# Seven wide block products for two token groups of the GLU layer, and all attention beside the first group

## The chip, the cores and the metric

One core of a Trainium2 chip runs the whole program. The metric is the device time of one execution in microseconds (us); less is better. The kernel before takes 665.15 us (median of 3 runs, 665.14 to 665.65). Engines are named as the profile names them: PE (TensorE matmuls), PEld (its weight loads), DVE (VectorE), ACT (ScalarE), POOL (GpSimd), SP (the queue that issues DMAs).

## The reference

Three layers follow each other on 1536 tokens of width 512 (2 batches of 768):

```python
# 1. attention, 8 heads of 64: a band of +-15 keys and one summary key (the maximum) per block of 32
x = softmax([masked local scores, summary scores + log(32)]) @ [v, block means of v]
# 2. normalisation and gated layer ("part 1"), d_ff 1536
xn = x / sqrt(mean(x * x) + 1e-6) * rms_g
y = (silu(xn @ w_gate) * (xn @ w_val)) @ w_out
# 3. second layer ("part 2"), d_ff 2048
h = y @ w_in
out = (h - tanh(h)) @ w_out2
```

All of it is fp32. The kernel gets near fp32 from the faster format fp32r by splitting each operand into a high and a low part: one fp32 product is three matmuls (high by high, high by low, low by high), made by `mm3` (lines 785 to 788).

## The kernel before

The 1536 tokens are 12 tiles of 128, in three groups of four tiles (`GROUPS`, line 44): a group is 512 columns of a matmul. The code counts groups from 0, so the change's "groups 2 and 3" are groups 1 and 2 here; the text below uses the code's numbers.

Nothing is issued by hand. Each piece of work is an `Op` of a planner with an engine, a planned duration, the operations that it follows, its buffers (`Slot`) and a due time; `Plan.order` runs a list schedule (the ready operation that may start least late goes first) and the instructions are emitted in that order, each engine's in its own fixed queue. The planner keeps DVE operations marked `port` and POOL operations from running at the same time, and `flex` lets it choose between DVE and POOL.

**Attention** is done in units, one per tile and half of the heads: 24 units, each with a load of 442 KB, scores, maxima on DVE, exponentials on ACT, transposes, values, and after the second half of a tile the normalisation, a transpose into columns and the split into `hi_t` (ACT) and `lo_t` (DVE) (`one_unit`). The 8 units of group 0 run first; the 8 of group 1 are due within group 0's part 1 and the 8 of group 2 within group 1's part 1 (lines 1237 to 1241).

**Part 1** runs the 12 slices f of d_ff (128 wide) for group 0, then all 12 for group 1, then all 12 for group 2: 36 calls of `step`, 2 of them cut in halves (`HEAD`). One step of 512 columns: gate and value, each 4 chunks of the contraction with `mm3` into one PSUM bank of the pool `mid` (2 banks), that is 24 matmuls; then tanh on ACT, two DVE operations for silu times value, a split into `hh`, `hl`; then 4 `mm3` into 4 accumulator banks (`bank`, 6 in all), 12 matmuls. Each step splits its weight slice again: `split` makes `ih`, `il` (gate and value) and `oh`, `ol` (output weights) with a cast on ACT and a subtraction on DVE or POOL (lines 761 to 763). The fp32 weights themselves are built once from their 64-bit packing by `widen` (a load of 512 KB, one ACT and two DVE operations per 512 columns).

**Part 2** does the same tokens in 3 groups of 8 pairs of slices (`pair`, lines 1101 on) and already uses seven block products of 256 columns in place of eight. `make_out` prepares its 16 output weight slices (due during group 1 of part 1, line 1244); `widen` of `w2` prepares its input weights, `make` forms their sums in the first group, `prepare` the sums of the tokens.

| planner pool | before | what holds it |
|---|---|---|
| `mid` | 2 PSUM banks | gate and value |
| `bank` | 6 PSUM banks | 4 accumulators, 2 for attention or part 2 |
| `raw` | 2 buffers of 512 KB | packed weights on their way to `widen`, `make_out` |

Of the kernel before, what the change touches and what calls it, by code (L numbers as in the profile page):

```python
# [52 lines left out]
AHEAD = 20.0  # L53
LAND = 1.0
# [4 lines left out]
def r32(ap):  # L59
    return ap.bitcast(F32)  # L60
# [201 lines left out]
def kernel(  # L262
# [20 lines left out]
    lo_r = [Region(const, f"lo{t}", NC_ * n * P, F32R) for t, n in GROUPS]  # L283
    hi_t = [r.get(F32R).rearrange("p (c s) -> p c s", c=NC_) for r in hi_r]
    lo_t = [r.get(F32R).rearrange("p (c s) -> p c s", c=NC_) for r in lo_r]
# [44 lines left out]
    buffers("il", 2, 1024, F32R)  # L330
    buffers("oh", 3, 512, F32R)
# [171 lines left out]
    def one_unit(t, hb, due, tag="att"):  # L503
# [185 lines left out]
        else:  # L689
# [19 lines left out]
            hi = act(0.48, lambda: nc.scalar.copy(cols(hi_t, t), wide()), co, slots=[px])  # L709
            lo = dve(0.62, lambda: nc.vector.tensor_tensor(cols(lo_t, t), wide(), r32(cols(hi_t, t)), ALU.subtract), hi, slots=[px], due=due + 4)  # L710
            ready_x[t] = [hi, lo]
# [9 lines left out]
    def w_second(f):  # L721
        return wd[0][:, f * 512:(f + 1) * 512]

    chain = {}
# [55 lines left out]
    wseq = [("a", f, 0, 0, half, f == 0, False) for f in range(HEAD)]  # L780
    wseq += [("a", f, 0, 0, n0, f == 0, f == NF1 - 1 and not HEAD) for f in range(HEAD, NF1)]
    wseq += [("a", f, 0, half, n0, False, f == HEAD - 1) for f in range(HEAD)]
    wseq += [("a", f, g, 0, GROUPS[g][1] * P, f == 0, f == NF1 - 1) for g in range(1, len(GROUPS)) for f in range(NF1)]
# [8 lines left out]
    first_ops = {}  # L792
    y_op = {}

    def step(k, at):

        kind, f, g, c0, c1, opens, closes = wseq[k]
        nm = f"{kind}{g}_{f}_{c0}"
        t0, nt = GROUPS[g]
        n = c1 - c0  # L800
        us = 0.694 * n / 512 + 0.004
        d, cut = w_first(f), 1024
        conv = wide_op.get((kind, f))
        eng = "pool"
        wh, wl, di = split(eng, d[:, :cut], cut, "i", conv)
        oh, ol, do = split(eng, d[:, cut:], 512, "o", conv and conv[cut // 512:])
        split_op.setdefault((kind, f), []).extend(o for a in di + do for o in a)
        pre = chain.get("first")
        mids = []
        for i in range(2 if kind == "a" else 1):  # L810
            m = bank("mid")
            mids.append(m)
            for c in range(NC_):
                def product(i=i, c=c, m=m):
                    s = slice((NC_ * i + c) * P, (NC_ * i + c + 1) * P)
                    mm3(
                        m[:, :n], wh[:, s], wl[:, s], hi_t[g][:, c, c0:c1], lo_t[g][:, c, c0:c1], c == 0, c == NC_ - 1
                    )

                if kind == "a":  # L820
                    need = [o for t in range(t0 + c0 // P, t0 + c1 // P) for o in ready_x[t]]
                else:
                    need = y_op[g][c]
                pre = pe(us, product, pre, *di[i], *need, slots=[m, wh, wl], due=at + (4 * i + c + 1) * us)
            mids[i].done = pre
        chain["first"] = pre
        first_ops.setdefault((kind, g), []).append(pre)
# [4 lines left out]
        ct = chain.get("th")  # L832
        m0 = mids[0]
        v = n / 512
        if kind == "a":
            a = act(0.05 + 0.43 * v, lambda: nc.scalar.activation(th[:, :n], m0[:, :n], AF.Tanh, scale=0.5), m0.done, ct, slots=[m0, th])
            chain["th"] = a
            a = dve(0.07 + 0.535 * v, lambda: nc.vector.scalar_tensor_tensor(th[:, :n], th[:, :n], 1.0, m0[:, :n], ALU.add, ALU.mult), a, slots=[m0, th])
            m1 = mids[1]
            a = dve(0.07 + 0.535 * v, lambda: nc.vector.tensor_tensor(th[:, :n], th[:, :n], m1[:, :n], ALU.mult), a, m1.done, slots=[m1, th])  # L840
        else:
            a = act(0.05 + 0.43 * v, lambda: nc.scalar.activation(th[:, :n], m0[:, :n], AF.Tanh), m0.done, ct, slots=[m0, th])
            chain["th"] = a
            a = dve(0.07 + 0.535 * v, lambda: nc.vector.tensor_tensor(th[:, :n], m0[:, :n], th[:, :n], ALU.subtract), a, slots=[m0, th])
        hi = act(0.09 + 0.43 * v, lambda: nc.scalar.copy(hh[:, :n], th[:, :n]), a, chain.get("hh"), slots=[th, hh])
        def rest(on):
            on.tensor_tensor(hl[:, :n], th[:, :n], r32(hh[:, :n]), ALU.subtract)

        ways = {"dve": (0.07 + 0.535 * v, lambda: rest(nc.vector), True)}
        if kind == "a" and g == 0:  # L850
            ways["pool"] = (0.1 + 1.2 * v, lambda: rest(nc.gpsimd), True)
        lo = flex(ways, hi, chain.get("hl"), slots=[th, hh, hl])
        chain["hh"], chain["hl"] = hi, lo
        if opens:
            acc[kind, g] = [bank("acc") for i in range(NC_ if kind == "a" else nt)]
        ps = acc[kind, g]
        nxt = at + 8 * us * (1 if kind == "a" else 0.5)
        if k + 1 < len(wseq):
            nxt += 8 * 0.694 * (wseq[k + 1][4] - wseq[k + 1][3]) / 512 * (1 if wseq[k + 1][0] == "a" else 0.5)
# [504 lines left out]
```

## Time and profile before

| | before |
|---|---|
| median of 3 runs | 665.15 us |
| the profiled execution's span, first to last instruction | 662.4 us |
| PE busy in the span | 651.8 us (98%), 3714 matmuls |
| DVE busy | 449.3 us (68%) |
| ACT busy | 334.2 us (50%) |
| POOL busy | 44.8 us (7%) |
| DMA | 136.5 MB, mean 206 GB/s |
| mean granted TensorE clock | 0.997 |

Busy time is what the instructions of an engine cover. A matmul row's duration holds the drain of its pipeline, so consecutive rows overlap and the distance from one start to the next is what a matmul costs the stream. The same holds for DVE and ACT rows that follow each other without a wait. The three steps of part 1 and the first group of part 2 are the stretches 42 to 176, 176 to 302, 302 to 398 and 398 to 484 us.

### The profile page before, as it was taken

How to read it: one execution, taken by the hardware profiler on the slowest of the kernel's cores; microseconds unless marked ns; L12 is line 12 of the kernel's file. 1: busy time of each engine (PE TensorE's matmuls, PEld its weight loads, DVE VectorE, ACT ScalarE, POOL GpSimd, SP SyncE). 2: the span in 40 equal slices, each digit the busy share in tenths (PEclk: the TensorE clock that was granted, in tenths of full speed). 3: DMA queues.
4: the chain of work that ended last, by engine and by line, in shares of the span. 5: the costliest groups of instructions: out<-in, count | busy, mean ns of one | idle time of the engine just before them, and what ended most of it. 6: DMA issues, size and time to landing. Idle time of an engine off the chain costs nothing.

```text
span 662.4 us, 10467 instructions
## 1 busy us (share of the span) xinstructions
PE 651.8 (98%) x3714; PEld 552.5 (83%) x3714; DVE 449.3 (68%) x1013; ACT 334.2 (50%) x688; POOL 44.8 (7%) x112
## 2 busy tenths in 40 slices
PE   8999999999999999999999999999999999999996
PEld 7998777888888888788888888888888888888885
DVE  5799986885857686779886456878584444544443
ACT  3995666774756565667554336544452231323222
POOL 2221222010110110000000000000000000000000
PEclk9999999999999999999999999999999999999998
DMA  9987664662365554350752066687678887898752
GB/s 344 334 289 257 201 189 140 198 196 82 103 208 174 165 162 145 128 159 13 246 147 87 0 232 246 244 310 271 208 255 287 268 283 265 290 318 287 245 172 96
DMA packets 52251, 136.51 MB, mean 206 GB/s; under 512 B 6200, under 2 KB 8680, under 8 KB 52200
## 3 DMA queue, kind: packets, MB, share of 16 engines
q1 hardware_dynamic: 52200, 135.86, 61.5%
q8 instruction: 29, 0.48, 0.3%
q14 instruction: 22, 0.18, 0.1%
HBM read 109.62 MB, written 26.21 MB: 205 GB/s over the span
## 4 chain that ended last, share of the span: by engine, by line
PE 88%; DMA 5%; DVE 3%; ACT 2%; SPq 0%; issue 0%; POOL 0%; ACTq 0%; DVEq 0%
PE bank L786 15%; PE bank L788 14%; PE bank L787 14%; PE mid L786 12%; PE mid L787 12%; PE mid L788 12%; PE bank L649 2%; PE bank L555 2%; PE bank L660 1%; DMA pad<-in_units_dram 1%; DMA raw<-in_w_dram 1%; PE bank L606 1%; DMA wd<-in_units_dram 1%; DMA wd<-in_ksum_dram 1%; DMA wd<-in_vsum_dram 1%; PE bank L700 1%
## 5 line engine op out<-in xcount | busy, mean ns | idle before, releaser
L786 PE MATMUL mid<-hi,ih 128*128 128x512 f32 (+1 forms) x304 | 121.1, 398 | 0.1
L787 PE MATMUL mid<-lo,ih 128*128 128x512 f32 (+1 forms) x304 | 116.9, 385 | 0.0
L788 PE MATMUL mid<-hi,il 128*128 128x512 f32 (+1 forms) x304 | 116.3, 383 | 0.0
L786 PE MATMUL bank<-oh,hh 128*128 128x512 f32 x192 | 75.8, 395 | 0.0
L788 PE MATMUL bank<-oh,hl 128*128 128x512 f32 x192 | 75.6, 394 | 0.0
L787 PE MATMUL bank<-ol,hh 128*128 128x512 f32 x192 | 75.4, 392 | 0.0
L786 PEld LDWEIGHTS mid<-hi,ih 128*128 128x128 f32 x304 | 57.2, 188 | 13.2 <-issue 2.2
L788 PEld LDWEIGHTS mid<-hi,il 128*128 128x128 f32 x304 | 57.1, 188 | 12.1
L787 PEld LDWEIGHTS mid<-lo,ih 128*128 128x128 f32 x304 | 57.3, 188 | 10.0
L786 PE MATMUL bank<-hh,oh 128*128 128x512 f32 (+1 forms) x152 | 60.5, 398 | 0.0
L761 ACT CAST ih<-wd 128x512 fp32r<-128x512 f32 x76 | 46.9, 619 | 24.0 <-PE mid L787 16.2
L787 PE MATMUL bank<-hl,oh 128*128 128x512 f32 (+1 forms) x152 | 58.3, 383 | 0.0
L788 PE MATMUL bank<-hh,ol 128*128 128x512 f32 (+1 forms) x152 | 58.1, 382 | 0.0
L763 DVE TENSOR_TENSOR il<-wd,ih 128x512 fp32r<-128x512 f32 x71 | 49.1, 697 | 3.6 <-ACT ih L761 3.3
L840 DVE TENSOR_TENSOR th<-th,mid 128x512 f32<-128x512 f32 (+1 forms) x38 | 25.0, 657 | 39.1 <-PE mid L788 38.6
L1155 ACT ACTIVATE lo<-lo 128x512 f32<-128x512 f32 (+1 forms) x48 | 25.0, 523 | 42.5 <-DVE lo L1134 42.5
L788 PEld LDWEIGHTS bank<-oh,hl 128*128 128x128 f32 x192 | 36.0, 188 | 9.1 <-DVE hl L1172 0.6
L744 ACT ACTIVATE wd<-raw 128x512 f32<-128x512 f32 x46 | 31.0, 676 | 24.4 <-DMA raw<-in_w_dram 23.7
L1155 ACT ACTIVATE lo<-mid 128x256 f32<-128x256 f32 x24 | 9.2, 384 | 64.8 <-PE mid L788 64.6
L787 PEld LDWEIGHTS bank<-ol,hh 128*128 128x128 f32 x192 | 36.0, 188 | 3.6
L786 PEld LDWEIGHTS bank<-oh,hh 128*128 128x128 f32 x192 | 36.2, 189 | 3.3
L583 ACT ACTIVATE pad<-pad,st 128x184 f32<-128x184 f32 x88 | 32.7, 442 | 9.9 <-DVE st L569 9.9
(172 smaller groups left out, 1455.1 us busy)
## 6 DMA issues: line engine op xcount, KB each, us to landing
raw<-in_w_dram SPq DMA_DIRECT2D x62, 512.0 KB, 3.9
wd<-ki SPq DMA_DIRECT2D x32, 512.0 KB, 5.9
wd<-ki SPq DMA_DIRECT2D x32, 384.0 KB, 5.0
oh<-ko SPq DMA_DIRECT2D x48, 256.0 KB, 2.9
ol<-ko SPq DMA_DIRECT2D x48, 256.0 KB, 3.5
pad<-in_units_dram SPq DMA_DIRECT2D x19, 442.0 KB, 4.4
ko<-hi SPq DMA_DIRECT2D x32, 256.0 KB, 2.7
ki<-ih SPq DMA_DIRECT2D x7, 512.0 KB, 4.0
```

What stands on the lines that cost most here:

```text
L555: nc.tensor.matmul(ps[e][:, j * SC:(j + 1) * SC], q[r, j], k[r, j], start=(j == 0), stop=(j == NP - 1), skip_group_check=True,)
L583: nc.scalar.activation(s, s, AF.Exp, bias=st[:, 0, h:h + 1], scale=-1.0)
L606: nc.tensor.transpose(pt[:, h * P:(h + 1) * P], sc[:, m0:m0 + P], ident)
L649: nc.tensor.matmul(av[:, h * (D + 1):(h + 1) * (D + 1)], ph[:, h * P:(h + 1) * P], v[:, h], start=(h == 0), stop=False, skip_group_check=True,
L744: a = act(0.58, lambda d=d, w=w: nc.scalar.activation(d, w(k=1).bitcast(F32), AF.Prelu, scale=2.0 ** -112, alpha=-(2.0 ** 32)), ld, *after ...
L761: a = act(0.52, lambda c=c: nc.scalar.copy(wh[:, c], d[:, c]), dep, chain.get(tag), slots=[wh])
L763: on.tensor_tensor(wl[:, c], d[:, c], r32(wh[:, c]), ALU.subtract)
L786: nc.tensor.matmul(o, ah, bh, start=first, stop=False, skip_group_check=True)
L787: nc.tensor.matmul(o, ah, bl, start=False, stop=False, skip_group_check=True)
L788: nc.tensor.matmul(o, al, bh, start=False, stop=last, skip_group_check=True)
L840: a = dve(0.07 + 0.535 * v, lambda: nc.vector.tensor_tensor(th[:, :n], th[:, :n], m1[:, :n], ALU.mult), a, m1.done, slots=[m1, th])
L1155: o = act(us, lambda: nc.scalar.activation(out(), x(), AF.Tanh), *after, slots=slots)
```

## The change

- Group 0 keeps its 12 steps, with the second halves of the first slices taken earlier (`BACK`). All 16 units of groups 1 and 2 are due beside it, the last `DONE` = 20 us before its end. Their columns are stored as plain fp32 (`xf_t`), not split.
- `combine` treats the columns of groups 1 and 2 as a 2 by 2 block matrix (contraction halves by groups) and forms four sums and seven split operands.
- `wide_pair` replaces the steps of groups 1 and 2, two slices f at a time: for gate and for value, seven products of 512 columns (each 2 chunks by `mm3`). Partial sums leave PSUM through `keep` (ACT) and `add` (DVE). The weight sums are formed by `wide_sums` and split by `wide_split`. Four results come out of a pair: two slices for group 1, whose output products follow in the pair, and two for group 2, which are kept in the space of used weights (`h_place`).
- `late_step` then does the 12 output products of group 2 from the kept results.
- `make_out` and `widen` of `w2` move: 10 `make_out` are due in the wide pairs, 6 in the late steps. `prepare` and `make` now wait for all wide products (`wide_ops`). Several buffers change place.

The core of the diff:

```diff
+BACK = 8
+DONE = 20.0
...
+    wseq = [(f, 0, half, f == 0, False) for f in range(HEAD)]
+    wseq += [(f, 0, n0, f == 0, f == NF1 - 1) for f in range(HEAD, NF1)]
+    wseq[BACK:BACK] = [(f, half, n0, False, False) for f in range(HEAD)]
...
-            lo = dve(0.62, lambda: nc.vector.tensor_tensor(cols(lo_t, t), wide(), r32(cols(hi_t, t)), ALU.subtract), hi, slots=[px], due=due + 4)
...
+                ready_x[t] = [act(0.52, lambda: nc.scalar.copy(cols(xf_t, t), wide()), co, slots=[px], due=due + 4)]
...
+    def combine(due):
...
+        def split_sum(n, b, after, slots=()):
...
+            for c in range(2):
...
+                x = act(0.6, lambda h=h, src=src: nc.scalar.copy(h(), src()), *after[c], *free, due=by, slots=slots)
+                z = both(0.66, lambda on, h=h, l=l, src=src: on.tensor_tensor(l(), src(), r32(h()), ALU.subtract), x, due=by, slots=slots)
...
+        s1 = split_sum(1, b11, x1)
+        s2 = split_sum(2, b21, x1)
+        t3 = tt("t", b22, b12, ALU.subtract, join(x2, un), [t])
+        t1 = tt(b12, b12, b11, ALU.subtract, join(t3, x1))
+        t2 = tt(b11, b11, "t", ALU.add, join(t3, t1, s1), [t])
+        s6 = split_sum(6, b11, t2)
+        s7 = split_sum(7, "t", join(t3, t2), [t])
+        s5 = split_sum(5, b12, t1)
+        s3 = split_sum(3, b22, join(x2, t3))
+        t4 = tt(b21, b21, b11, ALU.subtract, join(s2, t2))
+        s4 = split_sum(4, b21, t4)
...
+    def wide_sums(p, m):
...
+            o = flex(
+                {
+                    "pool": (0.66, lambda: nc.gpsimd.tensor_tensor(out(), x(), z(), op), True),
+                    "dve": (0.35, lambda: nc.vector.tensor_tensor(out(), x(), z(), op), True),
+                },
...
+        o1 = tt(lambda: s(1), lambda: a21, lambda: a22, ALU.add, *conv, *(wide_all if m else wide_rest), chain.get("sq"))
...
+        return sm, (
+            ((1, 2), lambda: d0, 512, [conv[0]], f0),
+            ((6, 7), lambda: sm[:, 0:512], 512, [o2, o3], None),
+            ((5, 3), lambda: sm[:, 512:1024], 512, [o1, o4], None),
+            ((4,), lambda: a22, q, [conv[1]], f1),
+        )
...
+    def wide_pair(p, at):
...
+        mx = [bank("mid") for m in range(2)]
+        my = [Slot(plan.pools["bank"], lambda t: t, lambda plan, now: 2) for m in range(2)]
...
+            out = (my if k in (2, 7, 4) else mx)[m]
...
+                for c in range(2):
+                    s = slice(w0 + c * P, w0 + (c + 1) * P)
+                    h, l = wide_x[k, c]
+                    mm3(out[:], wh[:, s], wl[:, s], h(), l(), opens and c == 0, closes and c == 1)
...
+        def keep(m, u, *after):
+            o = act(0.52, lambda: nc.scalar.copy(u[m][:], mx[m][:]), *after, *wide_first, slots=[u[m], mx[m]])
+            return o
+
+        def add(m, u, *after):
+            return dve(0.62, lambda: nc.vector.tensor_tensor(u[m][:], u[m][:], my[m][:], ALU.add), *after, slots=[u[m], my[m]])
+
+        two = range(2)
+        p1 = [product(1, m, True, False) for m in two]
+        u1 = [keep(m, ua, p1[m]) for m in two]
+        p2 = [product(2, m, True, True) for m in two]
+        c11 = [add(m, ua, u1[m], p2[m]) for m in two]
+        p6 = [product(6, m, False, False, u1[m]) for m in two]
+        u2 = [keep(m, ub, p6[m]) for m in two]
+        p7 = [product(7, m, True, False, c11[m]) for m in two]
+        p5 = [product(5, m, False, False, u2[m]) for m in two]
+        u4 = [keep(m, uc, p5[m]) for m in two]
+        c22 = [add(m, uc, u4[m], p7[m]) for m in two]
+        last = p == NF1 // 2 - 1
+        if not last:
+            p3 = [product(3, m, False, True, u4[m]) for m in two]
+        p4 = [product(4, m, False, True, c22[m]) for m in two]
...
+        c21 = [add(m, ub, u2[m], p4[m]) for m in two]
...
+        own(0, ua, c11)
+        h_op[f1] = silu(uc[0], uc[1], c22, lambda: h_place(f1), *gv_ops[f0])[1]
+        h_op[f0] = silu(mx[0], mx[1], p3, lambda: h_place(f0), *gv_ops[f0])[1]
+        own(1, ub, c21)
...
+    def late_step(k, f, at):
...
+        lo = halves(lambda: h_place(f), 1.0, lambda: hh[:], lambda: hl[:], h_op[f], ways=("dve", "pool"), slots=[hh, hl])
...
+            after2 = pe(MM, second, after2, lo, *do, slots=[oh, ol, hh, hl, ps[i]], due=at + (i + 1) * MM)
...
-        gate = first_ops["a", 0]
+        gate = gv_ops[1] + gv_ops[3]
...
+    for i in range(i0, 2 * NTILE):
+        a, z = begin + LEAD, at - DONE
+        unit(i // 2, i % 2, a + (z - a) * (i + 1 - i0) / (2 * NTILE - i0))
+    combine(at - 2.0)
...
+    for p in range(NF1 // 2):
+        wide_pair(p, at)
+        at += 14 * 2 * MM + 8 * MM
...
+    for i in range(10):
+        make_out(i, wide + (late - wide) * (i + 4) / 14)
...
+        widen_second(f)
+        if 10 + f < NF2:
+            make_out(10 + f, late + (at - late) * (f + 1) / 6)
```

## Rows read from the trace of the kernel before

**Rows 1.** The page: busy time by engine, and the chain that ended last by engine.

```profile
PE 651.8 (98%) x3714; PEld 552.5 (83%) x3714; DVE 449.3 (68%) x1013; ACT 334.2 (50%) x688; POOL 44.8 (7%) x112
PE 88%; DMA 5%; DVE 3%; ACT 2%; SPq 0%; issue 0%; POOL 0%; ACTq 0%; DVEq 0%
```

**Rows 2.** Stretches from:to, length, busy us (instructions) by engine, granted clock, DMA share, GB/s.

```profile
core 0: us, PE busy (x) PEld busy (x) DVE busy (x) ACT busy (x) POOL busy (x), PEclk, DMA share, GB/s
42.00:176.00 134.00, 133.47 (x756) 110.26 (x755) 111.69 (x259) 85.68 (x176) 24.25 (x54) 1.00 0.56 180
176.00:302.00 126.00, 126.00 (x662) 102.44 (x661) 90.52 (x208) 80.90 (x164) 12.64 (x23) 1.00 0.50 158
302.00:398.00 96.00, 96.00 (x415) 77.27 (x415) 68.26 (x122) 44.35 (x79) 0.00 (x0) 1.00 0.39 126
398.00:484.00 86.00, 85.55 (x540) 76.25 (x539) 65.23 (x141) 42.82 (x90) 0.00 (x0) 1.00 0.72 253
60.00:80.00 20.00, 20.00 (x111) 16.36 (x110) 19.49 (x42) 12.35 (x25) 4.91 (x6) 1.00 0.52 159
```

**Rows 3.** Whom PE waited for, whole span: total us, times, longest.

```profile
PE bank L555 <- POOL wd L527: 1.6, 2, 1.3
PE bank L786 <- DVE lo L1134: 0.6, 3, 0.3
```

**Rows 4.** Timeline of PE, group 2: each slice's first output matmul (start, duration).

```profile
307.90 0.39 PE L786 MATMUL bank<-hh,oh 128*128 128x512 f32 x1
316.31 0.39 PE L786 MATMUL bank<-hh,oh 128*128 128x512 f32 x1
324.71 0.39 PE L786 MATMUL bank<-hh,oh 128*128 128x512 f32 x1
```

**Rows 5.** Timeline of ACT: first accumulator read of group 0 and of group 2.

```profile
176.42 0.60 ACT L878 ACTIVATE lo<-bank 128x512 f32<-128x512 f32 x1 [1.80 <-PE bank L788]
398.43 2.67 ACT L878 ACTIVATE lo<-bank 128x512 f32<-128x512 f32 x4 [0.32 <-PE bank L788]
```

**Rows 6.** Timeline of DVE, rows that follow each other without a wait, 512 and 256 wide.

```profile
302.11 0.69 DVE L954 TENSOR_TENSOR pad<-lo,pad 128x512 fp32r<-128x512 f32 x1
302.71 0.68 DVE L938 TENSOR_TENSOR rest<-lo 128x512 f32<-128x512 f32 x1
...
309.89 0.42 DVE L1068 TENSOR_TENSOR rest<-wd 128x256 f32<-128x256 f32 x1
310.23 0.42 DVE L1090 TENSOR_TENSOR hi<-wd,hi 128x256 fp32r<-128x256 f32 x1
310.56 0.42 DVE L1069 TENSOR_TENSOR rest<-rest,wd 128x256 f32<-128x256 f32 x1
```

**Rows 7.** Groups of DVE instructions from 176 to 302 us, attention's eight units among them.

```profile
L569 DVE CUSTOM_DVE_ANT_0 pad<-bank,rest 128x184 f32<-128x184 f32 x32 | 9.2, 345 | 4.1 <-PE bank L555 4.0
L840 DVE TENSOR_TENSOR th<-th,mid 128x512 f32<-128x512 f32 x12 | 8.2, 687 | 13.5 <-PE mid L788 13.3
L677 DVE TENSOR_TENSOR pad<-bank,st 128x256 f32<-128x256 f32 x8 | 3.3, 417 | 0.0
L707 DVE SCALAR_TENSOR_TENSOR pad<-pad,st 128x512 f32<-128x512 f32 x4 | 3.0, 750 | 1.9 <-POOL st L696 1.9
L710 DVE TENSOR_TENSOR lo<-bank,hi 128x512 fp32r<-128x512 f32 x4 | 2.7, 685 | 1.4 <-ACT hi L709 1.4
```

**Rows 8.** Timelines of POOL and DVE around 72 us.

```profile
71.54 1.30 POOL L847 TENSOR_TENSOR hl<-th,hh 128x512 fp32r<-128x512 f32 x1 [3.27 <-ACT hh L845]
...
71.99 0.34 DVE L569 CUSTOM_DVE_ANT_0 pad<-bank,rest 128x184 f32<-128x184 f32 x1
72.26 1.13 DVE L763 TENSOR_TENSOR il<-wd,ih 128x512 fp32r<-128x512 f32 x1
```

**Rows 9.** The page's DMA issues: count, KB each, us to landing.

```profile
raw<-in_w_dram SPq DMA_DIRECT2D x62, 512.0 KB, 3.9
pad<-in_units_dram SPq DMA_DIRECT2D x19, 442.0 KB, 4.4
```

More of the change, by code (lines that the diff above doesn't have):

```diff
@@ L831, in step @@
         hl = slot("hl")
-        ct = chain.get("th")
-        m0 = mids[0]
+        m0, m1 = mids
         v = n / 512
[L835 to L853, printed above, removed]
@@ new lines, in step, with second @@
+        if opens:
+            acc[0] = [bank("acc") for i in range(NC_)]
+        ps = acc[0]
+        nxt = at + 8 * us
+        nxt += 8 * MM * (wseq[k + 1][2] - wseq[k + 1][1]) / 512 if k + 1 < len(wseq) else 0
+        after2 = chain.get("second")
+        for i in range(NC_):
+            def second(i=i):
+                s = slice(i * P, (i + 1) * P)
+                mm3(ps[i][:, c0:c1], oh[:, s], ol[:, s], hh[:, :n], hl[:, :n], opens, closes)
+            after2 = pe(us, second, after2, lo, *do, slots=[oh, ol, hh, hl, ps[i]], due=nxt + (i + 1) * us)
+            if closes:
+                outputs(0, i, ps[i], after2, *first_ops)
@@ new lines, in wide_split, with low @@
+    def wide_split(p, m, i, weights, sm, parts):
+            q = 2 * P
+            ks, src, n, of, f = parts[i]
+            wh, wl = slot("qh"), slot("ql")
+            ss = [wh, wl] + ([sm] if f is None else [])
+            v = n / 512
+            x = act(0.09 + 0.43 * v, lambda wh=wh, src=src, n=n: nc.scalar.copy(wh[:, :n], src()), *of, chain.get("q"), slots=ss)
+            def low(on, wh=wh, wl=wl, src=src, n=n):
+                on.tensor_tensor(wl[:, :n], src(), r32(wh[:, :n]), ALU.subtract)
+            z = flex(
+                {
+                    "dve": (0.07 + 0.535 * v, lambda low=low: low(nc.vector), True),
+                    "pool": (0.1 + 1.2 * v, lambda low=low: low(nc.gpsimd), True),
+                },
+                x,
+                chain.get("ql"),
+                slots=ss,
+            )
+            chain["q"], chain["ql"] = x, z
+            if f is not None:
+                gv_ops[f].extend((x, z))
+            else:
+                sq_ops.extend((x, z))
+            for i, k in enumerate(ks):
+                weights[k] = wh, wl, i * q, x, z
@@ new lines, with second @@
+    h_read = {}
+    def late_step(k, f, at):
+        oh, ol, do = out_weights(f)
+        hh, hl = slot("hh"), slot("hl")
+        lo = halves(lambda: h_place(f), 1.0, lambda: hh[:], lambda: hl[:], h_op[f], ways=("dve", "pool"), slots=[hh, hl])
+        h_read[f] = [chain["hh"], lo]
+        if not k:
+            acc[2] = [bank("mid" if i < 2 else "acc") for i in range(NC_)]
+        ps = acc[2]
+        after2 = chain["second"]
+        for i in range(NC_):
+            def second(i=i):
+                s = slice(i * P, (i + 1) * P)
+                mm3(ps[i][:], oh[:, s], ol[:, s], hh[:], hl[:], k == 0, k == NF1 - 1)
+            after2 = pe(MM, second, after2, lo, *do, slots=[oh, ol, hh, hl, ps[i]], due=at + (i + 1) * MM)
+            if k == NF1 - 1:
+                outputs(2, i, ps[i], after2, *tq_ops, *wide_all)
@@ L1097, in make @@
             at += m
+        if n:
+            after_a.extend([o1, o2, o3, o4] + [o for p in weights.values() for o in p[3:]])
         stored[n] = store
@@ L1214 @@
     at = START
-    for kind, f, g, c0, c1, _, _ in wseq:
+    for f, c0, c1, _, _ in wseq:
         times.append(at)
-        at += (12 if kind == "a" else 8) * 0.694 * (c1 - c0) / 512 + (SIDE if kind == "a" and g < 2 else 0.0)
-    begin = [next(t for t, w in zip(times, wseq) if w[0] == "a" and w[2] == g and w[1] >= (0 if g else HEAD)) for g in range(len(GROUPS))]
+        at += 12 * MM * (c1 - c0) / 512 + SIDE
+    begin = next(t for t, w in zip(times, wseq) if w[0] >= HEAD)
     summaries(0)
```

322 lines of the change are left out of this document (222 added, 100 removed).

## The prediction

> **What bounds the kernel now.** I read the page's busy times and its chain first, then the stretches, then PE's waits, then the spacing of single rows. PE covers 98% of the span and carries 88% of the chain that ended last [rows 1]. Busy PE alone proves little, since its rows overlap, so the next thing to see is whether PE ever stands still: the list of its waits names 1.6 us behind POOL and 0.6 us behind DVE as its largest items in the whole span [rows 3], and the granted clock is 1.00 in every stretch of part 1 [rows 2]. What a matmul costs the stream is the distance of starts: a slice f of group 2 takes 8.41 and 8.40 us from one first output matmul to the next [rows 4]. It holds 36 matmuls of 512 columns, so one costs 8.405 / 36 = 0.2335 us. From the first accumulator read of group 0 (176.42) to that of group 2 (398.43) are 222.0 us [rows 5]; 24 slices by 8.405 are 201.7, which leaves 20.3 us, 2.5 us for each of the eight attention units that run there. So the stretches are made of matmuls with almost nothing between them. DVE is second, and unevenly loaded: 111.7 of 134 us beside group 0, 90.5 of 126 beside group 1, 68.3 of 96 beside group 2, 65.2 of 86 in part 2's first group [rows 2].
>
> **What is removed from PE.** Per pair of slices, groups 1 and 2 now cost 2 groups x 2 slices x 2 (gate, value) x 4 chunks x 3 = 96 matmuls. The wide pair costs 2 x 7 products x 2 chunks x 3 = 84, of the same 512 columns. Twelve fewer in each of six pairs are 72, by 0.2335 us: 16.8 us. All of it lies on PE, which sets the end. Output products keep their number (24 a pair before; 24 after, 12 of them in the pair and 12 in the late steps), and so does attention; its units' 20.3 us of PE move from group 1's stretch to group 0's and cost nothing more in themselves.
>
> **What is added to DVE.** A DVE operation of 512 columns follows the one before it by 0.60 us, one of 256 by 0.33 to 0.34 [rows 6]; I take 0.605 and 0.335. Added: six adds a pair (c11, c22, c21, gate and value), 36 x 0.605 = 21.8; weight sums, eight a pair of 256 columns, 48 x 0.335 = 16.1; `combine`, 4 sums and 7 splits in halves, 22 x 0.605 = 13.3. Weight splits fall from 48 of 512 to 36 of 512 and 12 of 256, 3.2 less. Attention leaves the stretch with 9.2 + 3.3 + 3.0 + 2.7 = 18.2 us [rows 7]. From 90.5 + 68.3 = 158.8 [rows 2] that makes 158.8 - 18.2 + 21.8 + 16.1 - 3.2 + 13.3 = 188.6 us of DVE work, against 222.0 - 20.3 - 16.8 = 184.9 us of PE work in the wide and late stage. DVE was at 71% there and would be at 102%, were nothing moved out. Three things take it below: `combine` can run to some 10 us in group 0's last slices; POOL, which has nothing to do from 302 us on [rows 2], may take weight sums and splits; and the preparation of part 2 (`make_out`, `widen` of `w2`) can slide into part 2's first group, where 20.8 of 86 us are free.
>
> A full DVE is not by itself a stalled PE. From 60 to 80 us DVE is busy 19.49 of 20 us and PE 20.00 [rows 2], with none of the larger waits of rows 3. The order of the queues is what does it: the urgent operations go first and the weights have been split ahead. I take that as the nearest row for the wide stage, though it lasts 20 us and not 185.
>
> **Group 0's stretch.** Eight more units put 18.2 us of DVE, less four `lo` splits, on 111.7: about 128 of some 134 + 20.3 = 154 us, 83%, as much as the 83% now. ACT stands at 85.7 of 134 and gets some 23 us of attention (its 80.9 beside group 1 less 44.35 x 126 / 96, the rate beside group 2 [rows 2]): about 70%. The DMAs move too: eight loads of 442 KB [rows 9] are 3.5 MB more on SP's queue, over a stretch at 0.56 of the DMA engines and 180 GB/s: 23 GB/s more. Two attention banks serve 16 units in about 140 us, one per 8 to 9 us, where they served eight before. I put 0 here; the bounds are -2 (PE has more to pick from where the weights are late) and +4.
>
> **From group 0 to the wide pairs.** Product 6 waits for `keep` of product 1, and that for all of `combine` but its last operation, because the kept sums go where the columns lay; 14 of its operations, 8.5 us of DVE, wait for the last unit. Behind them on DVE stand the last slices' silu operations. Cover: the 20 us that the units are due ahead, at DVE free in about half, and products 1 and 2 of the first pair, 24 matmuls, 5.6 us. It just fits. 0 to 5 us, I take 1.
>
> **Inside a pair.** Gate and value alternate, so each hand-over has the other half's product as cover, 6 x 0.2335 = 1.4 us, or two products, 2.8 us. Tightest is product 5, `keep`, product 3: one product of cover against a copy of 0.60 us, by an ACT read of the same form [rows 5]. With one other ACT operation ahead it fits; with two it is late by some 0.4, for gate and value. Product 7 behind `add` has 2.8 us against 0.69, by the operation of the same form [rows 7]. At the end of a pair `mid` comes free only when silu has read both banks, three operations of 0.6 to 0.7 us after product 3; product 4 and the output products of the pair, 8.4 us of PE, lie in between. 0 to 0.8 us a pair, I take 0.4, six times: 2.4.
>
> **Into part 2.** `prepare` and `make` of the first group must wait for all wide products and so fall into the 33.6 us of the late steps, 11 operations of 0.605 us for `prepare` alone, beside 24 of the late steps' own splits, 21 us together; before, they were hidden in group 2. Behind them `widen` and `make_out` queue, on DVE and at the two `raw` buffers (3.9 us from issue to landing [rows 9]). 0 to 5 us, I take 1.
>
> **The sum.** Against the profiled execution: 662.4 - 16.8 + 0 + 1.0 + 2.4 + 1.0 = 650.0. The median lies 2.75 us above that span (665.15 against 662.4), so 652.8. With every cost at its upper bound it is 648.3 + 4 + 5 + 4.8 + 5 = 667.1, but they would not all fall together; two of them at the bound give 657 to 658. With all at the lower, 646.
>
> **Rivals.**
> *DVE sets the pace of the wide and late stage (slower).* The price is the shared port. While POOL ran a subtraction from 71.54 to 72.84, a DVE subtraction issued at 72.26 took 1.13 us in place of 0.68, though a DVE operation that reads PSUM ran through at 0.34 [rows 8]. If POOL takes the 48 weight sums at half of its 1.30 us each, DVE may lose 0.65 where its own would cost 0.335: 48 x 0.315 = 15 us more, 204 in all against 184.9 of PE. If nothing slides into part 2, PE is late by 19 us: 648.3 + 19 = 667, or 668 with the hand-overs' share. For it: 102% before any loss. Against it: DVE's adds and silu operations read PSUM, 8.5 us in each pair of 25 us, and leave room beside POOL; and the 20.8 us free in part 2. It decides from the point where the excess that can't slide passes 16.8 us.
> The Trainium skill, "SBUF — State Buffer", Who interferes with whom, says this of the port: DVE operations with two SBUF inputs and POOL operations that read SBUF exclude each other for a whole instruction. The trace agrees (1.13 against 0.68 us). By that rule POOL adds nothing to DVE's capacity for the added splits, and this rival stands or falls by how much of DVE's work reads PSUM.
> *Part of the excess stays.* DVE is full, most of the preparation slides, and PE waits at the pairs' ends or in part 2's first pairs for about 10 us: 648.3 + 10 = 658, 658 to 663.8. For it: part 2's first group has to take moved transfers besides at a DMA share of 0.72 [rows 2].
> *The gain doesn't arrive* (within 0.2%): units late by 15 us hold back `combine` and the pairs. Against it: 2.5 us of PE and 2.3 of DVE for each unit, in 8 us.
> *More than the matmuls:* group 0's stretch tightens by 2 us, below 648.3.
>
> **How the numbers follow.** About 0.2% (1.3 us) can be told from no change. Forecast, 648.3 to 658: 0.70, at 652.8. Below that: 0.03. Part of the excess stays: 0.12. The gain doesn't arrive: 0.04. DVE sets the pace: 0.11. Faster by over 0.2% takes the first three: 0.85; same 0.04; slower 0.11. The range reaches from 648 to 661: the forecast and the lower half of the partly lost gain.
>
> **What would show it.** After: 72 fewer PE matmuls; the granted clock 1.00; the wide pairs about 25.2 us apart (108 matmuls), DVE at 9 tenths or more in them with PE still at 9; PE's waits behind DVE or ACT below 5 us in all. Wrong: `product` waiting for `keep` or `add` in each pair; a DVE queue that is full through part 2's first group with PE waiting for `make`; a gap of several us where group 0 ends.

## The result, and the profile after

| | before | after |
|---|---|---|
| median of 4 runs each | 665.40 us (665.14 to 666.46) | 656.78 us (654.99 to 657.96) |
| ratio | | 0.9863, 95% interval 0.9841 to 0.9886 |
| span of the profiled execution | 662.4 us | 656.2 us |

The change is faster by 8.6 us, and 4.0 us short of the forecast of 652.8. The profiled execution of after is the longest of its four (657.96 us, 1.8 us around its span); that of before, with the 2.1 us that later runs of the same kernel have around their spans (664.48 for a span of 662.3), would be at 664.5, below its median. So the spans differ by 6.2 us where the medians differ by 8.6. What follows is read from the two spans; the 2.4 us between are these 0.3 us and the spread from run to run.

The page of after, busy time and the chain that ended last, as [rows 1] of before:

```profile
PE 638.7 (97%) x3642; PEld 541.8 (83%) x3642; DVE 486.4 (74%) x1087; ACT 357.3 (54%) x738; POOL 74.6 (11%) x136
PE 75%; DVE 9%; DMA 9%; ACT 3%; issue 2%; SPq 0%; POOL 0%; ACTq 0%; DVEq 0%; POOLq 0%
```

PE has 72 matmuls fewer, and its share of the chain has fallen from 88 to 75%: DVE's share has risen from 3 to 9%, DMA's from 5 to 9%. The stretches of after, columns as in [rows 2]: group 0; the last 21 us of group 0 and the wide pairs, whose first product starts at 196.77 us; the late steps; part 2's first group; the rest.

```profile
42.00:176.00 134.00, 132.59 (x853) 110.62 (x852) 108.49 (x309) 97.39 (x216) 36.39 (x76) 1.00 0.60 192
176.00:345.00 169.00, 168.84 (x739) 136.48 (x738) 151.24 (x258) 102.51 (x188) 30.06 (x25) 1.00 0.29 95
345.00:387.00 42.00, 41.01 (x187) 33.61 (x186) 37.49 (x70) 29.14 (x55) 0.00 (x0) 1.00 0.53 184
387.00:474.00 87.00, 81.47 (x498) 71.48 (x497) 71.70 (x157) 44.64 (x93) 0.00 (x0) 0.98 0.84 292
474.00:650.00 176.00, 175.69 (x1075) 154.13 (x1073) 85.74 (x181) 52.61 (x113) 0.00 (x0) 1.00 0.78 267
```

From the start of the first wide pair to the last products of the sixth:

```profile
197.00:347.00 150.00, 149.84 (x643) 120.65 (x642) 136.02 (x236) 90.38 (x165) 26.38 (x21) 1.00 0.32 106
```

In the wide pairs DVE is busy 136.02 of 150 us and PE 149.84: a DVE at nine tenths, and no stall. PE loses its time in one stretch, part 2's first group: 81.47 of 87 us, where before it was busy 85.55 of 86 [rows 2]. Of these stretches it is also the only one where the granted clock falls below 1.00, and the DMA share is 0.84 where it was 0.72.

The same in numbers that can be added up: for each PE row, the distance to the next start less what such a row costs a running stream (0.2335 us for 512 columns [rows 4], 0.1195 for 256, 0.09 to 0.105 for attention's small ones), summed by stretch. Some records are missing from a trace, so a sum is good to about 1 us.

| us beyond the matmuls' own pace | before | after | difference |
|---|---|---|---|
| 0 to 42 | 10.7 | 10.4 | -0.3 |
| 42 to 180, group 0 | 4.6 | 8.6 | +4.0 |
| 180 to 340, in after mostly the wide pairs | 2.8 | 0.2 | -2.6 |
| 340 to 380, in after the late steps | 0.0 | 0.7 | +0.7 |
| 380 to 460, part 2's first group | 0.7 | 8.4 | +7.7 |
| from 460 on | 1.0 | 1.5 | +0.5 |

The differences add up to +10.0, and with -16.8 for 72 matmuls to -6.8; the spans say -6.2. Of the 8.4 us in part 2's first group of after, 1.6 are matmuls at TensorE's lower clock, told in the last section. Among the runs below only the two that say so show that clock behind 42 us, so gaps of the others are to be set against 6.8.

Whom PE waited for, whole span (total us, times, longest), as [rows 3]:

```profile
PE bank L806 <- DVE lo L1402: 4.0, 4, 2.6
PE bank L560 <- POOL wd L532: 1.4, 2, 1.2
PE mid L1548 <- DVE idle L1543: 1.0, 1, 1.0
PE mid L806 <- DVE rest L1402: 0.9, 1, 0.9
PE bank L807 <- DVE hl L827: 0.8, 2, 0.7
PE bank L560 <- POOL st L700: 0.6, 1, 0.6
```

L1402 is the addition of partial sums in part 2's pairs. Its longest wait, 2.6 us, is the largest single loss of the whole span. Here is what stands before it, first SP's queue (the load is issued at 415.69), then ACT and DVE from their timelines (start, duration, engine, line, operation; in brackets the idle time before it and its releaser):

```profile
415.69 0.92 SPq L763 DMA_DIRECT2D raw<-in_w_dram  x1
...
423.83 0.66 ACT L765 ACTIVATE wd<-raw 128x512 f32<-128x512 f32 x1 [3.15 <-DMA raw<-in_w_dram]
...
424.52 0.43 DVE L766 TENSOR_SCALAR wd<-wd 128x512 uint32<-128x512 uint32 x1 [0.46 <-ACT wd L765]
424.86 0.42 DVE L1337 TENSOR_TENSOR wd<-wd,wd 128x256 f32<-128x256 f32 x1
425.19 0.69 DVE L767 SCALAR_TENSOR_TENSOR wd<-raw,wd 128x512 uint32<-128x512 uint32 x1
425.80 0.42 DVE L1356 TENSOR_TENSOR il<-wd,ih 128x256 fp32r<-128x256 f32 x1
426.13 0.41 DVE L1402 TENSOR_TENSOR lo<-up,bank 128x256 f32<-128x256 f32 x1
```

And PE's own timeline over the same time:

```profile
422.65 0.28 PE L808 MATMUL bank<-pad,il 128*128 128x256 f32 x1
422.77 0.28 PE L806 MATMUL bank<-pad,ih 128*128 128x256 f32 x1
...
423.60 0.40 PE L808 MATMUL bank<-oh,hl 128*128 128x512 f32 x1
426.60 0.43 PE L806 MATMUL bank<-pad,ih 128*128 128x256 f32 x1 [2.61 <-DVE lo L1402]
426.83 0.41 PE L807 MATMUL bank<-pad,ih 128*128 128x256 f32 x1
...
427.90 0.63 PE L806 MATMUL bank<-oh,hh 128*128 128x512 f32 x1
428.33 0.63 PE L807 MATMUL bank<-ol,hh 128*128 128x512 f32 x1
```

A packed weight of part 2 lands 8.12 us after its issue (to 423.80 in the chain of waits). ACT stands 3.15 us for it, then come `widen`'s ACT step and its two DVE steps, with `make` and a split between and behind them, and only then, on DVE's one queue, the addition that PE waits for. The packed loads of this stretch from the list of DMA issues, 387 to 474 us (form, count, KB each, median us to landing):

```profile
raw<-in_w_dram SPq DMA_DIRECT2D x9, 512.0 KB, 5.7
```

Nine such loads at a median of 5.7 us, 3.9 in the whole span of before [rows 9]. Before, none was issued in this stretch: the last went out at 352.5 us.

### The profile page after: what moved, and what is told of

Its sections match the earlier page's. It is cut to its first block, busy times and chain, and to the rows that moved or that the text cites. A ratio compares the mean times of both kernels' runs of the same rounds, so it can differ in the third digit from the quotient of the medians.

```text
span 656.2 us, 10503 instructions
## 1 busy us (share of the span) xinstructions
PE 638.7 (97%) x3642; PEld 541.8 (83%) x3642; DVE 486.4 (74%) x1087; ACT 357.3 (54%) x738; POOL 74.6 (11%) x136
## 4 chain that ended last, share of the span: by engine, by line
PE 75%; DVE 9%; DMA 9%; ACT 3%; issue 2%; SPq 0%; POOL 0%; ACTq 0%; DVEq 0%; POOLq 0%
PE bank L806 14%; PE bank L808 14%; PE bank L807 14%; PE mid L806 8%; PE mid L808 8%; PE mid L807 8%; DMA raw<-in_w_dram 5%; PE bank L654 3%; PE bank L560 2%; PE bank L665 1%; DMA out_dram<-th 1%; PE bank L611 1%; DVE wd L767 1%; DMA ki<-il 1%; DMA wd<-in_ksum_dram 1%
## 5 line engine op out<-in xcount | busy, mean ns | idle before, releaser
L806 PE MATMUL mid<-hi,ih 128*128 128x512 f32 (+1 forms) x136 | 54.0, 397 | 0.0
L806 PE MATMUL bank<-hh,oh 128*128 128x512 f32 (+1 forms) x128 | 50.2, 392 | 0.3 <-ACT hh L824 0.3
L808 PE MATMUL mid<-hi,il 128*128 128x512 f32 (+1 forms) x136 | 50.1, 368 | 0.0
L808 PE MATMUL bank<-hh,ol 128*128 128x512 f32 (+1 forms) x128 | 48.4, 378 | 0.0
L806 PE MATMUL mid<-pad,ih 128*128 128x512 f32 (+1 forms) x114 | 40.8, 358 | 0.2
L808 PE MATMUL mid<-pad,il 128*128 128x512 f32 (+1 forms) x114 | 40.6, 356 | 0.1
L807 PE MATMUL mid<-pad,ih 128*128 128x512 f32 (+1 forms) x114 | 40.6, 356 | 0.0
L807 PE MATMUL mid<-lo,ih 128*128 128x512 f32 (+1 forms) x112 | 40.6, 362 | 0.0
L1440 DVE TENSOR_TENSOR hl<-lo,hh 128x512 fp32r<-128x512 f32 x48 | 33.0, 688 | 8.2 <-ACT hh L1439 8.1
L1439 ACT CAST hh<-lo 128x512 fp32r<-128x512 f32 x48 | 29.8, 621 | 13.7 <-DVE lo L1427 13.6
L1427 DVE TENSOR_TENSOR lo<-lo 128x512 f32<-128x512 f32 (+1 forms) x48 | 26.5, 555 | 12.9 <-ACT lo L1423 12.9
```

The source lines that it names most:

```text
L806: nc.tensor.matmul(o, ah, bh, start=first, stop=False, skip_group_check=True)
L807: nc.tensor.matmul(o, ah, bl, start=False, stop=False, skip_group_check=True)
L808: nc.tensor.matmul(o, al, bh, start=False, stop=last, skip_group_check=True)
L1427: return dve(us, lambda: nc.vector.tensor_tensor(out(), x(), z(), ALU.subtract), *after, slots=slots)
L1439: h = act(0.52, lambda j=j: nc.scalar.copy(hh[j][:], th[j][:]), *of, chain.get("hh"), slots=[th[j], hh[j], hl[j]])
L1440: l = dve(0.62, lambda j=j: nc.vector.tensor_tensor(hl[j][:], th[j][:], r32(hh[j][:]), ALU.subtract), h, slots=[th[j], hh[j], hl[j]], port ...
```

## The experiments

Theory A: PE's loss in part 2 comes of packed weights (`widen` of `w2`) that slide from the wide and late stage into part 2's first group and land late there. Against it stand, in the expectations' other letters and words, that the move of `make_out` costs in itself, that transfers crowd each other, that DVE or the shared port holds the wide pairs back, and that the loss lies with the units beside group 0. Each run is compared with the kernel before on its own chip (medians 665.45 for the first four, 664.93 for the next four, 665.82 for the last three); the interval of the ratio is in brackets, and "gaps" are the table's measure for 380 to 460 us: 0.7 before, 8.4 after.

**The planner reserves 6 us for the landing of part 2's packed weights** (behind the 1.5 us of the transfer itself; in after 1 us for `widen`, 4 us for `make_out`). Orders change, no work does.

```diff
+  ..., slots=[raw], land=6.0 if nm[0] == "b" else LAND)     # widen
-        ld = dma(0.524, ..., chain.get("raw"), slots=[raw], land=FAR)   # make_out
+        ld = dma(0.524, ..., chain.get("raw"), slots=[raw], land=6.0)
```

> The changed kernel, except that the planner is told that the packed weights of part 2 land 6 us after the transfer's own time (1 us for the input weights, 4 us for the output weights before). Only the order of the queues changes. Theory A (PE waits some 9 us in part 2's first group because DVE and ACT stand in their fixed order before weights that land later than planned): those waits fall below 4 us and the time to 650 to 653 us. Theory B (DVE has more work there than it can do, wherever it stands in the queue): waits and time as in the changed kernel, 655 to 658 us.

Measured: 655.77 us, 0.9845 [0.9828, 0.9862]: within the spread of after. Gaps 6.8, as in after without its lower clock. Nine loads remain in 387 to 474 us, landing in 5.5 us at the median; the 2.6 us wait is gone, but PE now waits 1.2 and 0.8 us for ACT's copies (L1406). Told of the landing alone, the order only spreads the waits: A's gain did not come this way.

**The same order with packed loads of half the size** (256 KB in place of 512 for part 2's weights; the second half of each is left out).

```diff
-  nc.sync.dma_start(raw[:], src[:, 2 * o:2 * o + 1024])
+  nc.sync.dma_start(raw[:, 0:k], src[:, 2 * o:2 * o + k])   # k = 512 for w2
-  nc.sync.dma_start(raw[:], src[:, 1024:2048])
+  nc.sync.dma_start(raw[:, 0:512], src[:, 1024:1536])
```

> The changed kernel in the same order of instructions, but each transfer of part 2's packed weights brings 256 KB in place of 512 KB, and the other half of the buffer keeps what was in it (part 2's weights are therefore not the reference's). Theory A (late landing): PE's waits in part 2's first group fall from 9 to below 4 us, time 650 to 653 us. Theory B (DVE's amount of work): no change, 655 to 658 us.

Measured: 649.58 us, 0.9757 [0.9734, 0.9779], 7.2 us below after. Gaps 3.0. The loads from 387 to 474 us, from the view of one tile (us to landing):

```profile
L763 SPq DMA_DIRECT2D raw<-in_w_dram x7: 333/333/371, 390.8 to 418.4; - x7
DMA to landing us min/median/max: 3.0/3.4/6.0
```

PE's busy time in that stretch is 85.34 us, where after has 81.47 (columns as in [rows 2]):

```profile
387.00:474.00 87.00, 85.34 (x525) 74.62 (x524) 75.82 (x165) 47.28 (x98) 0.00 (x0) 1.00 0.83 286
```

The planned order and the instructions of every compute engine are the same; the bytes of these 32 loads (16 of `widen`, 16 of `make_out`) alone are worth 7 us, the lower clock of after's profiled run (1.6 us) among them. This is what shows theory A's core.

**Halving other transfers instead**: the stores of part 2's prepared input weights write half (the other half isn't stored).

```diff
+  elif pick:
+      here, there = r32(s[:, :n]).rearrange("p (a m) -> p a m", a=2), r32(k[:, :n // 2])...
+  else:
+      here, there = r32(s[:, :n // 2]), r32(k[:, :n // 2])
```

> The changed kernel in the same order, but the stores of part 2's input weights write half of the columns, and the loads of them in the later groups read that half twice (results not the reference's). This takes some 6 MB out of the DMA engines in part 2's first group and leaves the loads of packed weights as they are. If those land late (5.7 us in the median against 3.9 us) because the engines are crowded, they land in about 4 us, PE's waits there fall from 9 to below 5 us and the time to 650 to 653 us. If their own size decides, no change: 655 to 658 us.

Measured: 655.32 us, 0.9849 [0.9819, 0.9879]. The DMA share from 387 to 474 us falls from 0.84 to 0.75, the loads' median landing from 5.7 to 5.0 us, the gaps to 5.5 (6.8 in after at the full clock); the time can't be told from after's. Crowding has a part in the landing, but relieving the queue of other bytes does not bring what halving the late loads brings.

**The kernel before with `make_out` due later**, 30 to 110 us after group 2's begin.

```diff
-                make_out(f, begin[1] + (begin[2] - begin[1]) * (f + 1) / NF2)
+                make_out(f, begin[2] + 30.0 + 80.0 * (f + 1) / NF2)
```

> The kernel before with one part of the change alone: the 16 preparations of output weights are due beside group 2's part 1 in place of group 1's. Nothing is added to DVE. Theory A (what costs is that the loads crowd into the end of part 1 and part 2's first group, land late and stand ahead of urgent work): 2 to 5 us slower than before, 667 to 670 us, with PE waiting between 398 and 450 us. Theory B (it costs only together with the added DVE work of the wide products): within 1 us of before.

Measured: 664.77 us (10 runs), 0.9983 [0.9974, 0.9993]: no loss, if anything a gain of 1 us; gaps 0.7. I had expected a loss here, and missed. But the run hardly tests it, since the work did not move: a due time does not hold an operation back, and the list schedule took the work up about as early as before. The 16 loads of `make_out` go out from 145.2 to 274.9 us (145.3 to 264.8 in before, 171.4 to 377.9 in after), the last of `widen` at 360.4 us (352.5 in before), and DVE is busy 24.92 of the 42 us that end at 387 (23.30 in before, 37.49 in after). Whether the move of `make_out` costs something in itself stays open; the nine packed loads in part 2's first group of after are all `widen`'s.

**The kernel before with all 16 units beside group 0.**

```diff
-        if g + 1 < len(GROUPS):
...
+        if g == 0:
+            a, z = begin[0] + LEAD, begin[1] - 6.0
+            for i in range(8, 24):
+                unit(i // 2, i % 2, a + (z - a) * (i - 7) / 16)
```

> The kernel before with the other moved part alone: all 16 attention units of the second and third group beside group 0's part 1. If attention costs nothing more in the first stretch: 664 to 666.5 us. If the first stretch overfills: above 667 us, with PE waits before 200 us.

Measured: 667.01 us (10 runs), 1.0028 [1.0015, 1.0041]: 1.6 us slower. Gaps from 42 to 180 us are 9.7 (4.6 before), from 180 to 340 none (2.8 before). The timelines of PE and DVE at its largest gap:

```profile
71.45 0.63 PE L606 MATMUL bank<-ident,pad 128*128 128x128 f32 x4 [1.22 <-DVE st L569]
...
68.72 2.04 DVE L455 TENSOR_TENSOR wd<-wd 128x768 f32<-128x768 f32 x1
70.69 0.34 DVE L569 CUSTOM_DVE_ANT_0 pad<-bank,rest 128x184 f32<-128x184 f32 x1
```

A unit's maxima (L569) stand behind a preparation step of 2.04 us on DVE's queue. The same step took 0.95 us in before (at 62.05); here a weight split on POOL (L763) ran from 68.39 to 69.95 us beside it. The crowding of the units is a cost of its own, and after pays it too: +4.0 in group 0 against -2.6 where the units left.

**Room on DVE in the wide pairs**: the 48 weight sums are left out, the products take weights as they lie.

```diff
+        return None, (
+            ((1, 2), lambda: d0, 512, [conv[0]], f0),
+            ((6, 7), lambda: d1, 512, [conv[1]], f1),
...
```

> The changed kernel without the 48 weight sums: products 6, 7, 5 and 3 take the weights themselves, so the gate and value results of the second and third group are not the reference's; everything else is there, and the transfers keep their size. It frees 48 x 0.335 = 16 us of DVE (or twice that of POOL) in the wide pairs. If part 2's packed weights come late because DVE has no room for them in the wide pairs, fewer than the 9 loads fall into part 2's first group, PE's waits there fall below 5 us, and the time to 649 to 653 us. If they come late for another reason (two buffers, the gate on the place for the results), 655 to 658 us as in the changed kernel.

Measured: 658.29 us, 0.9885 [0.9857, 0.9913], not faster. DVE has 132.1 of 165 us from 180 to 345 and the nine loads stay where they were (395.2 to 440.7 us, median 5.8). Gaps in part 2's first group fall to 4.8, but 5.3 appear in the wide pairs, 3.5 of them in one wait behind a `silu` operation on DVE and most of the rest at the lower clock behind it. So room in the pairs does not pull the loads forward; on the time the run is inconclusive, since the new order has a stall of its own.

**The weight sums on DVE alone**, none on POOL.

```diff
-                    "pool": (0.66, lambda: nc.gpsimd.tensor_tensor(out(), x(), z(), op), True),
```

> The changed kernel with the weight sums on DVE alone (POOL may still take splits). If POOL's share of the sums gave DVE room, the wide pairs get tighter: 1 to 5 us slower than the changed kernel. If POOL's hold on the shared port cost DVE as much as it saved, within 1.5 us of the changed kernel, or faster.

Measured: 658.75 us (7 runs, 655.83 to 662.63), 0.9912 [0.988, 0.9945]. Gaps in the wide pairs 2.1 in place of 0.2, in part 2's first group 7.1, with a stretch at the lower clock as in after. Without POOL's help it is, if anything, 2 us slower; the intervals overlap. POOL's share of the sums is no loss. Nor is the loss in part 2 due to the shared port: POOL is busy 0.00 us from 345 us on in after.

**Room on DVE in the late steps**: their 24 subtractions for the low parts are left out (the high parts are used for both).

```diff
-        oh, ol, do = out_weights(f)
-        hh, hl = slot("hh"), slot("hl")
...
+        w = act(0.52, lambda: nc.scalar.copy(oh[:], w_first(f)[:, cut1:]), ...)
+        lo = act(0.52, lambda: nc.scalar.copy(hh[:], h_place(f)), ...)
+        ol, hl, do = oh, hh, [w]
```

> The changed kernel, whose late steps leave out the low parts: the 24 subtractions on DVE (12 of the output weights, 12 of the kept results) are not made and the high parts are multiplied in their place (the second group of tokens to be finished is then not near fp32). It frees 24 x 0.605 = 14.5 us of DVE between the wide pairs and part 2, where DVE is busy 35.9 of 40 us. If the packed weights of part 2 come late because DVE is full in the late steps, at most 5 loads in place of 9 fall into part 2's first group, PE's waits there fall below 4 us, time 648 to 652 us. If the places that they are written to or the two buffers hold them, 9 loads and 655 to 658 us as in the changed kernel.

Measured: 650.59 us, 0.9778 [0.9753, 0.9803]. The stretches that [rows 2] has for before, here the late steps and part 2's first group:

```profile
345.00:387.00 42.00, 40.97 (x190) 33.72 (x188) 28.99 (x57) 31.70 (x60) 0.00 (x0) 1.00 0.71 251
387.00:474.00 87.00, 85.65 (x535) 76.13 (x535) 73.39 (x160) 45.52 (x96) 0.00 (x0) 1.00 0.81 285
```

DVE falls from 37.49 to 28.99 us in the late steps, six of `widen`'s loads are issued there in place of two, five in place of nine in part 2 (median landing 4.7 us), and the gaps are 2.0. So the full DVE of the late steps is what pushes loads into part 2, as far as one run with an order of its own can show it. The prediction's 21 us, for 24 splits of the late steps and 11 operations of `prepare`, are this work.

**Truer times and due times for the planner**: 4 us for `widen`'s landing, 6 for `make_out`'s, 2 for the stores and later loads of the prepared weights, and `make_out` due earlier.

```diff
+  ..., land=4.0 if nm[0] == "b" else LAND)     # widen
+  ..., slots=[s], land=2.0)                    # stores and loads of prepared weights
-        make_out(i, wide + (late - wide) * (i + 4) / 14)
+        make_out(i, wide + (late - wide) * (i + 4) / 16)
```

> The changed kernel in another order: the planner is told landings near the measured ones for part 2 (4 us after the transfer for packed input weights, 6 us for packed output weights, 2 us for the kept weights), and the ten output weights in the wide pairs are due two sixteenths of that stage earlier. If the order is what exposes the late landings, 650 to 654 us with PE's waits in part 2's first group below 6 us. If any order must wait for them, 655 to 658 us.

Measured: 651.89 us (651.57 to 652.98), 0.9799 [0.9776, 0.9821], 4.9 us below after. Gaps 3.9, though still nine loads at a median of 5.4 us in part 2. This is what an order alone can do; that the waits now lie where less stands behind them is my reading, not shown by itself. Which of the edits does it was not taken apart.

**Two places for the prepared output weights in place of one**, with the same truer times: `make_out` forms its low part in place, so that its two buffers become two complete places, and 13 of its 16 calls go ahead of the input weights, 11 in the second run.

```diff
-    plan.pools["os"] = Buffers([wd[0][:, 3 * W1 + i * 512:3 * W1 + (i + 1) * 512] for i in range(2)])
-    plan.pools["op"] = Buffers([wd[0][:, W1:W1 + 1024]])
+    plan.pools["os"] = Buffers([wd[0][:, a:a + 1024] for a in (W1, 3 * W1)])
...
-            on.tensor_tensor(o[:, 512:].bitcast(F32R), d[:], o[:, :512], ALU.subtract)
+            on.tensor_tensor(o[:, :512].bitcast(F32R), o[:, :512], o[:, 512:], ALU.subtract)
...
-    for i in range(10):
+    for i in range(13):
```

> A version meant to be faster: the order with landings near the measured ones, and two places in place of one for a prepared output weight (the low part is written over the fp32 value, so the same memory holds two), with thirteen output weights ahead of the input weights. If the loads' place in the order and the single place are what is left to gain, 649.5 to 652 us, and no slower than the kernel with the landings alone (651.9). If the loads' landing decides whatever the order, 653 to 657 us.

> The same with eleven output weights ahead of the input weights in place of thirteen. Within 1 us of the kernel with thirteen if the number doesn't matter; more if single late loads decide.

Measured: 649.41 us, 0.9761 [0.9743, 0.978] with 13, 649.35 us, 0.9765 [0.9746, 0.9784] with 11: the number doesn't matter. Both are 16.4 us faster than before and some 7 us faster than after. The late steps and part 2's first group of the first:

```profile
345.00:387.00 42.00, 41.75 (x199) 34.95 (x198) 38.48 (x73) 29.89 (x56) 0.00 (x0) 1.00 0.56 191
387.00:474.00 87.00, 86.15 (x534) 75.89 (x535) 74.52 (x163) 47.46 (x98) 0.00 (x0) 1.00 0.86 300
```

Its packed loads from 387 to 474 us, from the view of one tile:

```profile
L763 SPq DMA_DIRECT2D raw<-in_w_dram x6: 332/352/381, 396.7 to 429.9; - x6
DMA to landing us min/median/max: 5.6/6.2/7.4
```

And all of PE's waits from 380 to 460 us:

```profile
PE bank L806 <- DVE lo L1402: 0.8, 3, 0.3
```

PE is busy 86.15 of 87 us again, at a DMA share of 0.86, above after's, and with loads that land no sooner (median 6.2 us). Six of them lie there with 13 ahead and eight with 11 (median 6.1 us), at the same time for the kernel, so neither their number nor their landing decides: the order leaves room for the landing. A high DMA share and slow landings are thus no loss by themselves. What the fast runs have in common is that PE waits little for the additions in this stretch: 1.5 us with half loads, 1.3 without the late splits, 0.8 and 1.0 in these two, 5.3 in after. The two versions differ from the one with truer times in the places, the number ahead and the due times at once; which of them brings the last 2.5 us was not taken apart.

## Why the prediction came out as it did

Direction and mechanism held; the loss sits in one term, which I sized too small. In the spans, what lies beside the 72 matmuls came to +10.0 us by the table, for +4.4 in the sum. That the two larger misses, the pairs (2.4 too much) and part 2 (6.7 too little), have opposite signs is luck.

- **72 matmuls, -16.8 us.** Held: 3642 for 3714, 72 fewer, and each costs what it did (108 in 25.2 us, next item).
- **The pairs' hand-overs, +2.4.** Too high: there are none to speak of. One pair follows the other at the distance that I gave, 108 matmuls, 25.2 us, in the timeline of PE (the same product of two successive pairs):

```profile
205.14 0.40 PE L806 MATMUL mid<-pad,ih 128*128 128x512 f32 x1
...
230.37 0.40 PE L806 MATMUL mid<-pad,ih 128*128 128x512 f32 x1
```

- **Group 0's stretch, 0 (bounds -2 to +4), and the hand-over to the wide pairs, +1.** The stretch got +4.0, its upper bound, and the stage after it -2.6, which I had not counted: the units had left gaps beside group 1 (2.8 us in the table) that vanish with them, as they do in the run that moves the units alone. Together +1.4, near the 1 that the sum had, but by luck: two terms of opposite sign, neither of them the hand-over. The units alone cost 1.6 us by the run with nothing else changed. DVE's mean share came as forecast (125.34 of the 155 us from 42 to 197, 81% for 83%) and did not tell of the loss; the one wait taken apart came from a long operation ahead of an urgent one. Of after's 8.6 us there the list of waits names 1.2, so what makes up the rest is not shown. No wait was found where `combine` ends.
- **Into part 2, +1 (bounds 0 to 5).** This is the step that failed: +7.7, beyond its bound. I named the queueing at the `raw` buffers and DVE's late steps, but sized a load by 3.9 us, a median over a span in which all but the first five are issued at a DMA share of 0.40 to 0.64; at 0.84 the median is 5.7 and the longest 8.1. I also took the cost as DVE's time, where the price is what stands in order behind the late operation, and left out that the clock can fall when PE stands (1.6 of the 7.7 us, below).
- **Rivals.** "Part of the excess stays", 658 to 663.8 with PE waiting in part 2's first pairs, names the place rightly and is about 1 us too slow; the time lies in the forecast's own range, 648.3 to 658. "DVE sets the pace" fell: its price is real, its place does not decide. While POOL worked for 3.45 us, DVE's rows read:

```profile
204.06 3.45 POOL L784 TENSOR_TENSOR ol<-wd,oh 128x512 fp32r<-128x512 f32 x2
...
204.57 0.67 DVE L1077 TENSOR_TENSOR lo<-lo,bank 128x512 f32<-128x512 f32 x1
205.17 1.19 DVE L1025 TENSOR_TENSOR il<-lo,ih 128x512 fp32r<-128x512 f32 x1
206.28 0.68 DVE L1077 TENSOR_TENSOR lo<-lo,bank 128x512 f32<-128x512 f32 x1
206.88 1.19 DVE L1102 SCALAR_TENSOR_TENSOR th<-th,lo 128x512 f32<-128x512 f32 x1
```

  Operations with two SBUF inputs take 1.19 us for 0.68; the additions with one input in PSUM, which hold PE's banks, run through at 0.67 and 0.68. The split of weights was ahead by enough. The Trainium skill, "SBUF — State Buffer", Who interferes with whom, draws the line in the same place: outside DVE's two-port modes, a DVE instruction with at most one SBUF input doesn't contend with GpSimd (POOL). My argument against this rival was misread, though: of the 8.5 us in each pair that I took to read PSUM, only the six additions and two of the eight silu operations do, 8 x 0.605 = 4.8 us; the other six read kept sums in SBUF, as the last row above does.
- **What was to show it.** 72 fewer matmuls, the pairs' distance and DVE's nine tenths came. PE's waits behind DVE or ACT "below 5 us in all" did not: behind the additions of part 2 alone are 5.4 us. The sign that I gave for a failure, a DVE full through part 2's first group, was the wrong one: it was busy 71.70 of 87 us there. Two readings of the rows were incomplete, without weight for the sum. Before's list of waits also has 1.0 us at the program's start, more than the 0.6 that I named as second, and after has the same 1.0. And attention's 18.2 us on DVE left out two smaller groups of its operations (2.7 and 1.4 us).

What stays open: why the planner places `widen` so late was read from the code (one place for `make_out`'s result, one chain for all packed loads) and from the runs that change it together with the times; the places were not changed alone. A third `raw` buffer, which would test the prediction's other place of queueing, was not tried.

## What to carry to other kernels

When a change fills an idle engine, look for the work that used that idle time, follow it to the stretch where it now falls, and price its loads at that stretch's DMA share, not at the page's median. Cost a late load by the urgent operations that stand behind its consumers on in-order queues. In the wide pairs an engine at nine tenths fed PE without a gap, since what PE waits for went first.

## What was not expected of the hardware

Here a wait of PE cost more than its length. After the gap of 2.6 us TensorE ran at its lower clock (the windows of after before, around and behind the gap; the clock stands after the five busy times):

```profile
420.00:423.00 3.00, 3.00 (x17) 2.56 (x16) 2.57 (x7) 0.67 (x2) 0.00 (x0) 1.00 1.00 395
423.00:426.00 3.00, 0.99 (x6) 0.51 (x4) 2.54 (x7) 1.69 (x3) 0.00 (x0) 1.00 0.94 323
426.00:429.00 3.00, 2.40 (x9) 2.20 (x10) 2.27 (x5) 1.95 (x4) 0.00 (x0) 0.63 0.98 317
429.00:432.00 3.00, 3.00 (x22) 2.90 (x21) 2.04 (x5) 1.37 (x4) 0.00 (x0) 0.80 0.60 194
```

The granted clock of 0.63 and 0.80 are means over 3 us that hold both levels. From 426.60 to 430.0 eleven matmuls of 256 columns start 0.215 us apart in place of 0.12 (422.65 to 422.77 in PE's timeline above), and three of 512 take 0.425 (427.90 to 428.33) in place of 0.2335: 11 x 0.096 + 3 x 0.19 = 1.6 us on top of the 2.6. That is the level of 1.2 in place of 2.4 GHz. The Trainium skill, "TensorE: Matmul & The Clock Gate", Part 1: The HAM clock gate, gives 426.7 ns from start to start of 512 columns at the lower clock, and the rows agree (0.425); its 215.7 ns at the full clock is less than the 0.2335 us of [rows 4].

Two other runs show the same. In the run without the weight sums, the wait of 3.5 us in the wide pairs is followed by a granted clock of 0.66 from 329 to 334 us. With the sums on DVE alone, a wait of 2.1 us for an addition in part 2's first group is followed by 0.84 and 0.59 in the two windows of 3 us from 426 us on. The other runs, whose waits there are shorter, keep 1.00 from 387 to 474 us.
